# A drain, two orders of gathers, transposes and sums moved in a kernel of attention and routed experts

## The chip, the core and the metric

The kernel runs on one core of one Trainium2 chip. The metric is the device time in microseconds (us) of one execution. The engines have short names in the profile: PE is TensorE (PEld its weight loads), DVE is VectorE, ACT is ScalarE, POOL is GpSimd, SP is SyncE. A "q" behind a name means the engine's sequencer, which waits and issues DMAs.

## The reference

Eight batches of eight heads go through attention that is causal in blocks of 64 rows; the result, as rows of 512, goes through a layer of eight experts in which each row is sent to one expert.

```python
B, H, S, D = (8, 8, 576, 64)                       # attention
scores = scale * np.matmul(q, k.transpose(0, 1, 3, 2))
mask = block_i >= block_j                          # blocks of 64
attn = np.exp(scores - max) / (sum + 1e-09)
x = np.matmul(attn, v)                             # -> (B, S, 512)
...
logits = np.einsum('bsd,de->bse', x, w_gate)       # E = 8 experts, F = 1024
local_gate = sigmoid(x @ w_local)
for s in range(S):
    fresh_e = argmax(logits[b, s])
    e = fresh_e if s == 0 or local_gate[b, s] < 0.5 else prev_e
    h = np.maximum(x[b, s] @ w1[e], 0.0)
    out[b, s] = softmax(logits[b, s])[e] * (h @ w2[e])
```

## The kernel before

**First stage, attention.** The loop over `i` from 0 to 31 takes one pair of heads per slot (`NPAIR` is 32, `HP` is 4 pairs per batch). TensorE's order in slot `i` is written out by hand: the products with the values of the pair before (`values(i - 1)`, L932), the scores of this pair in three units (L894) with the last block of 64 (`last_scores`, L917), the transposes of keys and queries of the next pair (`transposes(i + 1)`: eight of 128 rows, L856, and one of the tail, the last 64 rows of keys and of queries, L860), and then what the slot has of tasks: gate logits, sums, turning the result back into rows, steps of the routing. Slots 1 and 3 have no tasks. Slot 1 has another order (`swap`): its scores come first, then the values of pair 0, then the transposes, then the sums.

ScalarE makes the exponentials (L904, L921), copies the eight transposed blocks from PSUM into `qkT` (L851; in slot 0 VectorE does that) and the output of the values out of `po` (L936). VectorE adds the exponentials of the column blocks into S (`add_chunks`, L944), so that one product with ones later gives the sums, and copies the tail (L862). GpSimd clears the corners above the diagonal (L881), rearranges the loaded keys and queries (L822) and issues the loads of the experts' weights. The PSUM tile `po` of 1024 columns is shared: columns 0 to 127 take the tail's transpose, 128 to 191 and 832 to 895 the scores of the last block, 256 to 831 the output of the values. The tiles named `sc` rotate through three buffers; scores, the eight transposes (`kq`) and the tasks take them in turn.

**The routing** (which row goes to which expert, at which place) is a generator of small steps, most of them VectorE's. `steps.vector(w)` issues steps until their written weights reach `w`; `steps.tensor()` issues one that needs TensorE. The steps of slot 25's end are `steps.vector(2.7)`, those at slot 26's start `steps.vector(1.4)` after the sums of pair 25.

**Second stage, the experts.** The rows are grouped in tiles of 128 with one expert each, 15 tiles of a first group (rows of the first five batches) and 28 of a second group whose row numbers are only known some time into this stage; of these 43, 38 run always and 5 stand behind a branch. For tile `i`: GpSimd gathers its rows from DRAM into `xg` (six buffers; L654), SyncE issues a transposing DMA into `xT` (L1218), VectorE copies the expert's first matrix (L1205), TensorE multiplies (L1006, 32 products), ScalarE applies the Relu (L1009), TensorE multiplies with the second matrix (L1155, 8 products), ScalarE scales the result into `y` (three buffers; L1160), and GpSimd stores it row by row with an indirect DMA (L1162). On TensorE the second matrix of tile `i - 1` follows the first of tile `i`. GpSimd's queue runs in program order. In the first group the order per iteration is: store of tile `i - 1`, then the gather of tile `i + 5`, which takes the buffer of tile `i - 1`. The gathers of tiles 0 to 3 are issued in the attention stage, those of 4 and 5 in iteration 0, and behind them stands `nc.gpsimd.drain()` (L1281), which holds GpSimd's queue until what is before it is done. A second drain stands before the branch (L1295). From the second group on the gather of tile `i + 4` stands ahead of the store.

SyncE's queue holds, in program order too, the loads, the stores of attention rows and of routing factors (L676, L680), and the transposing DMAs. The order around the gathers in an iteration of the second stage:

```python
gathers(i + AHEAD, relu[0] if i > NS[0] + 1 else None)
second_mm(*tiles[i - 1], done, ev.pop(i - 1), factor_of(xgs[(i - 1) % NX]))
...
if i < NS[0] + 1:
    gathers(i + NX - 1)
if i == 0:
    nc.gpsimd.drain()
if i + 2 >= AHEAD:
    rows_of(i + 2)
```

Here `AHEAD` is 4, `NX` 6 and `NS[0]` 15.

Of the kernel before, what the change touches and what calls it, by code (L numbers as in the profile page):

```python
# [62 lines left out]
def kernel(  # L63
# [11 lines left out]
    nc = tc.nc  # L75
# [14 lines left out]
    P = 128  # L90
# [119 lines left out]
    def factor_of(x):  # L210
        return x[:, XH:]
# [562 lines left out]
    with tc.tile_pool(name="atn_const", bufs=1) as cst, \  # L774
# [78 lines left out]

        def turn_part(i, part, ps):
            for j in range(4):
                nc.tensor.transpose(ps[:, j * P:j * P + P],  # L856
                                    raws[i][1 + part][:, j].rearrange("s h d -> s (h d)"), id_f)
# [6 lines left out]

        def transposes(i, copy):
            if i >= NPAIR:
                return
            ps = psp.tile([P, 2, 512], F32, tag="sc", name="kq")
            for part in range(2):
                turn_part(i, part, ps[:, part])  # L870
            back_in_order(i, slice(0, 2), ps, copy)
            turn_tail(i)

# [186 lines left out]
        wload = 0  # L1060

        def behind(i):

            values(i - 1)
            if not swap:
                add_chunks(i - 1)
            load_v(i + 1)
            steps.vector(1.4)

        for i in range(NPAIR):  # L1070
# [18 lines left out]
            for u in range(len(UNITS)):  # L1089
                exps(i, u, scores(i, u))  # L1090
                if u == 0:
                    last_scores(i)
                    if i == 0:
                        transposes(1, nc.vector.tensor_copy)
                        constants()
                        for h in range(2):
                            hs = slice(64 * h, 64 * h + 64)
                            nc.sync.dma_start(
                                out=wg2[hs, :, 16 * h:16 * h + E],
                                in_=moe_w_gate.rearrange("(p h d) e -> h d p e", h=2, d=D)[h])  # L1100
                            nc.sync.dma_start(
                                out=wg2[hs, :, 16 * h + E:16 * h + E + 1],
                                in_=moe_w_local.rearrange("(p h d) e -> h d p e", h=2, d=D)[h])
            if swap:
                behind(i)
            if i:
                transposes(i + 1, nc.scalar.copy)
            if swap:
# [14 lines left out]
            steps.tensor()  # L1123
            if i < NPAIR - 1:
                steps.vector(2.7)
# [9 lines left out]
        slot[0] = NPAIR  # L1135


        values(NPAIR - 1)
# [8 lines left out]
    with tc.tile_pool(name="ffn_s", bufs=2, reuse_waits="tile") as f_p, \  # L1147
# [3 lines left out]

        def second_mm(ph, j, hT, ev, factor, y=None):
            ps = f_ps.tile([P, Dm], F32, tag="ps_y", name="ps_y")
# [4 lines left out]
            if y is None:  # L1158
                y = f_p.tile([P, Dm], F32, tag="y", name="y", bufs=3)
            nc.scalar.activation(y, ps, func=AF.Copy, scale=factor)  # L1160

            st = nc.gpsimd.indirect_dma_start(  # L1162
# [51 lines left out]
        def rows_of(i):  # L1214

            if i < len(tiles):
                xT = f_p.tile([P, KO1, P], BF16, tag="xT", name="xT", bufs=3)
                ended["DMA", len(ended)] = nc.sync.dma_start(  # L1218
                    out=xT, in_=row_of_x(xgs[i % NX]), transpose=True)
                xTs[i] = xT  # L1220
# [39 lines left out]
        for i, (ph, j) in enumerate(tiles):  # L1260
# [10 lines left out]
            if i:  # L1271
                point()

                gathers(i + AHEAD, relu[0] if i > NS[0] + 1 else None)
                second_mm(*tiles[i - 1], done, ev.pop(i - 1), factor_of(xgs[(i - 1) % NX]))


            if i < NS[0] + 1:
                gathers(i + NX - 1)
            if i == 0:  # L1280
                nc.gpsimd.drain()  # L1281
            if i + 2 >= AHEAD:
# [54 lines left out]
```

## Time and profile before

| what | us |
|---|---|
| runs of the kernel | 432.31, 431.83, 432.20 |
| their median | 432.2 |
| the profiled execution, its own time | 433.36 |
| its span, from the first to the last instruction | 431.6 |
| granted TensorE clock over the span | 1.00 |

The profile is one execution. Its times are us from the start of the span. A row of the timeline gives start, duration, engine, line, operation, tiles and shapes, a count, and in brackets the idle time of the engine before it with the one who ended it. That name is inferred from semaphores: where an engine waits for several, the profile names the one that came last. Matmuls are pipelined, so neighbouring rows of TensorE overlap a little.

By stage (busy us of each engine; a view of stretches): the attention up to 280.6 us, the stretch to the row of TensorE that waits, that stretch, and the rest:

```profile
core 0: us, PE busy (x) PEld busy (x) DVE busy (x) ACT busy (x) POOL busy (x), PEclk, DMA share, GB/s
0.00:280.60 280.60, 276.71 (x2657) 203.22 (x2657) 179.89 (x411) 183.95 (x292) 87.53 (x237) 1.00 0.87 175
280.60:312.00 31.40, 30.94 (x349) 21.77 (x348) 26.33 (x82) 12.75 (x22) 13.48 (x11) 1.00 0.65 132
312.00:314.00 2.00, 0.43 (x8) 0.47 (x9) 1.97 (x5) 0.69 (x1) 1.70 (x2) 1.00 0.82 179
314.00:432.00 118.00, 112.04 (x1275) 81.41 (x1271) 47.14 (x63) 59.07 (x94) 83.86 (x61) 1.00 0.55 136
```

### The profile page before, as it was taken

The numbers are of one execution on the slowest core, as the hardware profiler recorded it, in microseconds if no ns is written. First come the engines' busy times: TensorE is split into PE (matmuls) and PEld (weight loads), VectorE is DVE, ScalarE is ACT, GpSimd is POOL, SyncE is SP. The second block draws the span as 40 slices with busy tenths as digits, with TensorE's granted clock in tenths as the row PEclk, the third lists the DMA queues.
The fourth block names the chain that finished last, engine by engine and source line by source line (L and its number), as shares of the span: only waits on it lengthen the run. The fifth ranks groups of instructions, "written<-read, shape, count | busy, mean of one in ns | idle before, by whom it ended". The sixth has DMA issues, their size and how long they took to land. (4 is left out here: it accounts for less than half of the span.)

```text
span 431.6 us, 11727 instructions
## 1 busy us (share of the span) xinstructions
PE 420.1 (97%) x4282; PEld 306.9 (71%) x4282; DVE 255.3 (59%) x557; ACT 256.5 (59%) x409; POOL 186.6 (43%) x309
## 2 busy tenths in 40 slices
PE   8999999999999999999999999999999999999995
PEld 7677767767677776676776777667677777777763
DVE  3353565466365566968789976898788433333320
ACT  4668657766776677656676557634444555555553
POOL 2324522232222223314223234304875788888843
PEclk9999999999999999999999999999999999999999
DMA  7568699799899789796989979993686465664541
GB/s 183 124 161 184 119 215 169 154 212 213 176 185 204 167 159 196 162 139 150 225 142 218 192 161 170 182 146 86 159 189 141 132 148 147 142 154 139 142 107 74
DMA packets 114360, 69.78 MB, mean 162 GB/s; under 512 B 77567, under 2 KB 106751, under 8 KB 114304
## 3 DMA queue, kind: packets, MB, share of 16 engines
q1 hardware_dynamic: 96896, 38.07, 39.1%
q0 software_dynamic: 17408, 30.96, 37.2%
q8 instruction: 36, 0.59, 0.6%
q14 instruction: 20, 0.16, 0.1%
HBM read 66.88 MB, written 14.70 MB: 189 GB/s over the span
## 5 line engine op out<-in xcount | busy, mean ns | idle before, releaser
L944 DVE TENSOR_TENSOR S<-S,Pc 128x896 f32<-128x896 f32 (+3 forms) x128 | 90.5, 707 | 16.9 <-PE o L932 8.7
L894 PE MATMUL sc<-qkT 64*128 64x288 f32 (+3 forms) x768 | 98.7, 389 | 0.4 <-ACT qkT L1054 0.3
L894 PEld LDWEIGHTS sc<-qkT 64*128 64x128 f32 x768 | 68.7, 187 | 14.1 <-ACT qkT L1054 0.5
L1205 DVE COPY w1c<-w_bf 128x4096 bf16 x36 | 44.4, 1232 | 55.4 <-PE ps_h L1006 52.2
L1006 PEld LDWEIGHTS <-w1c 128*128 128x128 bf16 x1152 | 67.2, 98 | 10.7 <-DVE x L765 2.0
L1162 POOL DMA_INDIRECT out_dram<-y,idx x38 | 60.2, 1584 | 28.4 <-ACT hT L1009 12.5
L1155 PE MATMUL ps_y<-w_bf,hT 128*128 x304 | 71.7, 379 | 0.0
L1006 PE MATMUL ps_h<-xT,w1c 128*128 128x128 bf16 x1088 | 66.3, 219 | 2.5 <-DMA xT<-xg 1.6
L936 ACT COPY oT<-o 128x576 f32<-128x576 f32 x32 | 20.5, 639 | 80.0 <-PE o L932 77.7
L904 ACT ACTIVATE Pc<-sc 128x448 f32<-128x448 f32 (+1 forms) x96 | 63.9, 707 | 0.0
L851 ACT COPY qkT<-kq 128x1024 f32<-128x1024 f32 x30 | 63.4, 2112 | 0.4 <-PE kq L856 0.4
L1009 ACT ACTIVATE hT<-ps_h 128x512 bf16<-128x512 f32 x76 | 45.2, 597 | 24.5 <-PE ps_h L1006 24.5
L932 PE MATMUL o<-Pc,v 128*64 128x320 f32 (+2 forms) x512 | 57.4, 366 | 0.0
L822 POOL COPY w_bf<-w_bf 128x512 f32<-128x512 f32 x61 | 41.8, 702 | 33.2 <-DMA w_bf<-in_k_dram 19.5
L654 POOL DMA_INDIRECT xg<-x_rows,idx x38 | 43.1, 1133 | 22.9 <-DVE w1c L1205 10.9
L1160 ACT ACTIVATE y<-ps_y,xg 128x512 f32<-128x512 f32 x38 | 26.2, 689 | 43.8 <-PE ps_y L1155 35.1
L932 PEld LDWEIGHTS o<-Pc,v 128*64 128x64 f32 x512 | 35.1, 137 | 23.6
L904 ACT ACTIVATE S<-sc 128x576 f32<-128x576 f32 x64 | 41.6, 650 | 15.3 <-PE sc L894 15.2
L1155 PEld LDWEIGHTS <-hT 128*128 128x128 bf16 x304 | 28.2, 98 | 27.7 <-issue 0.5
L881 POOL MEMSET Pc<- 64x128 f32 x96 | 17.5, 200 | 65.5 <-ACT Pc L904 61.2
L881 POOL MEMSET S<- 64x128 f32 x32 | 6.4, 199 | 91.0 <-ACT S L904 90.0
L862 DVE COPY qkT<-o 128x128 f32<-128x128 f32 x32 | 9.2, 288 | 55.2 <-PE o L860 55.0
(287 smaller groups left out, 453.1 us busy)
## 6 DMA issues: line engine op xcount, KB each, us to landing
w_bf<-in_moe_w_dram POOLq DMA_DIRECT2D x16, 1024.0 KB
w_bf<-in_k_dram SPq DMA_DIRECT2D x32, 256.0 KB, 4.2
w_bf<-in_q_dram SPq DMA_DIRECT2D x32, 256.0 KB, 4.2
v<-in_v_dram SPq DMA_DIRECT2D x64, 128.0 KB, 3.3
x_rows<-xg SPq DMA_DIRECT2D x24, 128.0 KB, 3.1
qkl<-in_k_dram SPq DMA_DIRECT2D x32, 32.0 KB, 3.4
qkl<-in_q_dram SPq DMA_DIRECT2D x32, 32.0 KB, 4.2
vl<-in_v_dram SPq DMA_DIRECT2D x32, 32.0 KB, 8.9
```

The lines of the kernel that those rows point to most:

```text
L654: st = nc.gpsimd.indirect_dma_start(out=x, out_offset=None, in_=x_dram[:rows], in_offset=bass.IndirectOffsetOnAxis(ap=row_of(ph, j), axis= ...
L822: copies[j](m, raws[i][1 + j].rearrange("p h j d -> p j h d"))
L851: copy(qkTs[i % 2][:, parts, :512].rearrange("p a (s j) -> p a j s", j=4), ps.rearrange("p a (j s) -> p a j s", j=4))
L894: nc.tensor.matmul(ps[:, h, col:col + n], lhsT=t[r, 0, c * P:c * P + P], rhs=t[r, 1, q0:q0 + n], start=True, stop=True)
L904: nc.scalar.activation(exps_at(i, c, q0, n, rows), ps[rows, :, col:col + n], func=AF.Exp, scale=scale_attn)
L932: nc.tensor.matmul(po[64 * h:64 * h + 64, VO + q0:VO + q0 + n], lhsT=vv, rhs=exps_at(i, c, q0, n, slice(0, P))[:, h, :], start=(c == 0), s ...
L944: nc.vector.tensor_add(Ss[i][rows, :, P * c:], Ss[i][rows, :, P * c:], Pc[i % 2][rows, :, POS[c]:POS[c] + n])
L1006: nc.tensor.matmul(ps[:, fo, :], lhsT=w[:, ko * F + f0:ko * F + f0 + P], rhs=xT[:, ko, :], start=(ko == 0), stop=(ko == KO1 - 1))
L1009: relu[0] = nc.scalar.activation(hT[:, half * (FO // 2):(half + 1) * (FO // 2), :], ps, func=AF.Relu)
L1155: nc.tensor.matmul(ps, lhsT=hT[:, fo, :], rhs=w2_bf[:, bass.ds(ev + fo * Dm, Dm)], start=(fo == 0), stop=(fo == FO - 1))
L1162: st = nc.gpsimd.indirect_dma_start(out=out_flat, out_offset=bass.IndirectOffsetOnAxis(ap=row_of(ph, j), axis=0), in_=y, in_offset=None, b ...
L1205: ended["w"] = nc.vector.tensor_copy(w, w1_bf[:, bass.ds(ev[i], WE)])
```

## The change

Five edits.

1. The transpose of the tail moves ahead of the eight others (`ahead` 0: first; 6 in slot 1: behind six of them; 8 in slot 0: behind all eight as before). VectorE's copy of the tail moves with it, and in slot 0 this copy now stands ahead of VectorE's copy of the eight.
2. The routing steps worth 2.7 at the end of slot 25 move to slot 26, behind the sums of pair 25.
3. GpSimd's first drain moves from behind the gathers of tiles 4 and 5 to a place ahead of the values of the last pair, that is ahead of these gathers.
4. In the first group the gather of tile `i + 5` stands ahead of the store of tile `i - 1`, behind ScalarE's scaling. The gathers of tiles 4 and 5 stay in iteration 0.
5. `xT` has five buffers instead of three.

```diff
@@ -851,8 +851,8 @@
             copy(qkTs[i % 2][:, parts, :512].rearrange("p a (s j) -> p a j s", j=4),
                  ps.rearrange("p a (j s) -> p a j s", j=4))
 
-        def turn_part(i, part, ps):
-            for j in range(4):
+        def turn_part(i, part, ps, js=range(4)):
+            for j in js:
                 nc.tensor.transpose(ps[:, j * P:j * P + P],
                                     raws[i][1 + part][:, j].rearrange("s h d -> s (h d)"), id_f)
 
@@ -862,14 +862,18 @@
             nc.vector.tensor_copy(qkTs[i % 2][:, :, 512:S],
                                   po[:, TAIL:TAIL + P].rearrange("p (a s) -> p a s", a=2))
 
-        def transposes(i, copy):
+        def transposes(i, copy, ahead=0):
             if i >= NPAIR:
                 return
             ps = psp.tile([P, 2, 512], F32, tag="sc", name="kq")
-            for part in range(2):
-                turn_part(i, part, ps[:, part])
+
+
+            for j in range(9):
+                if j == ahead:
+                    turn_tail(i)
+                if j < 8:
+                    turn_part(i, j // 4, ps[:, j // 4], (j % 4,))
             back_in_order(i, slice(0, 2), ps, copy)
-            turn_tail(i)
 
         def exps_at(i, c, q0, n, rows):
             if c == 0:
@@ -1059,12 +1063,17 @@
         arrange(1, (nc.vector.tensor_copy, nc.gpsimd.tensor_copy))
         wload = 0
 
+
+        SUMS_FIRST = 26
+
         def behind(i):
 
             values(i - 1)
             if not swap:
                 add_chunks(i - 1)
             load_v(i + 1)
+            if i == SUMS_FIRST:
+                steps.vector(2.7)
             steps.vector(1.4)
 
         for i in range(NPAIR):
@@ -1091,7 +1100,7 @@
                 if u == 0:
                     last_scores(i)
                     if i == 0:
-                        transposes(1, nc.vector.tensor_copy)
+                        transposes(1, nc.vector.tensor_copy, 8)
                         constants()
                         for h in range(2):
                             hs = slice(64 * h, 64 * h + 64)
@@ -1104,7 +1113,7 @@
             if swap:
                 behind(i)
             if i:
-                transposes(i + 1, nc.scalar.copy)
+                transposes(i + 1, nc.scalar.copy, 6 if swap else 0)
             if swap:
                 add_chunks(i - 1)
             for x in pending.pop(0) if pending else []:
@@ -1121,7 +1130,7 @@
                 w_next = weights_at(qkT.rearrange("p j a s -> p (j a s)").bitcast(BF16)[:, :WE],
                                     ev[1])
             steps.tensor()
-            if i < NPAIR - 1:
+            if i < NPAIR - 1 and i != SUMS_FIRST - 1:
                 steps.vector(2.7)
             arrange(i + 2, [nc.gpsimd.tensor_copy] * 2)
 
@@ -1135,6 +1144,8 @@
         slot[0] = NPAIR
 
 
+        nc.gpsimd.drain()
+
         values(NPAIR - 1)
         add_chunks(NPAIR - 1)
         steps.all()
@@ -1149,7 +1160,7 @@
                      reuse_waits="tile") as f_ps:
         banks["of"] = lambda nm: f_ps.tile([P, 512], F32, tag="rt", name=nm, bufs=3)
 
-        def second_mm(ph, j, hT, ev, factor, y=None):
+        def second_mm(ph, j, hT, ev, factor, y=None, between=lambda: None):
             ps = f_ps.tile([P, Dm], F32, tag="ps_y", name="ps_y")
             for fo in range(FO):
                 nc.tensor.matmul(ps, lhsT=hT[:, fo, :],
@@ -1158,6 +1169,7 @@
             if y is None:
                 y = f_p.tile([P, Dm], F32, tag="y", name="y", bufs=3)
             nc.scalar.activation(y, ps, func=AF.Copy, scale=factor)
+            between()
 
             st = nc.gpsimd.indirect_dma_start(
                 out=out_flat,
@@ -1214,7 +1226,7 @@
         def rows_of(i):
 
             if i < len(tiles):
-                xT = f_p.tile([P, KO1, P], BF16, tag="xT", name="xT", bufs=3)
+                xT = f_p.tile([P, KO1, P], BF16, tag="xT", name="xT", bufs=5)
                 ended["DMA", len(ended)] = nc.sync.dma_start(
                     out=xT, in_=row_of_x(xgs[i % NX]), transpose=True)
                 xTs[i] = xT
@@ -1272,13 +1284,12 @@
                 point()
 
                 gathers(i + AHEAD, relu[0] if i > NS[0] + 1 else None)
-                second_mm(*tiles[i - 1], done, ev.pop(i - 1), factor_of(xgs[(i - 1) % NX]))
-
-
-            if i < NS[0] + 1:
-                gathers(i + NX - 1)
-            if i == 0:
-                nc.gpsimd.drain()
+
+
+                second_mm(*tiles[i - 1], done, ev.pop(i - 1), factor_of(xgs[(i - 1) % NX]),
+                          between=lambda: i < NS[0] + 1 and gathers(i + NX - 1))
+            else:
+                gathers(NX - 1)
             if i + 2 >= AHEAD:
                 rows_of(i + 2)
 
```

## The prediction

> **What bounds the kernel now.** The page's busy line comes first, then the view of waits for TensorE alone: who it waited for, total us, times, longest us.
>
> ```profile
> span 431.6 us, 11727 instructions
> PE 420.1 (97%) x4282; PEld 306.9 (71%) x4282; DVE 255.3 (59%) x557; ACT 256.5 (59%) x409; POOL 186.6 (43%) x309
> ...
> PE ps_h L1006 <- DMA xT<-xg: 1.6, 1, 1.6
> PE ps_h L1006 <- ACTq L1297: 0.8, 1, 0.8
> PE rtr L364 <- ACT qkT L851: 0.8, 2, 0.4
> ...
> PE o L932 <- POOL w_bf L822: 0.4, 1, 0.4
> PE o L932 <- POOL Pc L881: 0.4, 1, 0.4
> ...
> PE trg L704 <- DVE S L944: 0.2, 1, 0.2
> ```
>
> TensorE is the bound from end to end: all its idle time is 431.6 - 420.1 = 11.5 us. The change removes no arithmetic, so it can gain only what stands in such rows, and it can lose by making new ones. Every term below is therefore a TensorE wait that goes, stays, or comes. Two rows are out of reach: the 0.8 us at L1297 is the branch near the end, which is not touched, and the chain of waits after TensorE's last product is not either.
>
> **The long wait, 1.57 us.** The timeline around it (start, us, engine, line; in brackets the idle time before and who ended it), with GpSimd's DMAs, ScalarE's first two y, the transposing DMA of tile 7 and the drain (its duration, then its start):
>
> ```profile
> 313.57 1.95 PE L1006 MATMUL ps_h<-xT,w1c 128*128 128x128 bf16 x32 [1.57 <-DMA xT<-xg]
> ...
> 308.17 1.21 SPq L1218 DMA_TRANSPOSE xT<-xg  x1
> ...
> 291.18 1.48 POOL L654 DMA_INDIRECT xg<-x_rows,idx  x1 [10.88 <-DVE w1c L1205]
> 292.96 1.00 POOL L654 DMA_INDIRECT xg<-x_rows,idx  x1 [0.30 <-issue]
> 298.56 1.02 POOL L1162 DMA_INDIRECT out_dram<-y,idx  x1 [4.60 <-ACT hT L1009]
> 299.89 1.02 POOL L654 DMA_INDIRECT xg<-x_rows,idx  x1 [0.30 <-issue]
> ...
> 303.44 1.02 POOL L654 DMA_INDIRECT xg<-x_rows,idx  x1 [0.30 <-issue]
> ...
> L1281 POOLq DRAIN  x1: 6135/6135/6135, 291.5 to 291.5; - x1
> ...
> 291.04 0.69 ACT L1160 ACTIVATE y<-ps_y,xg 128x512 f32<-128x512 f32 x1 [0.27 <-PE ps_y L1155]
> ...
> 295.44 0.69 ACT L1160 ACTIVATE y<-ps_y,xg 128x512 f32<-128x512 f32 x1 [1.13 <-PE ps_y L1155]
> ```
>
> The gathers of tiles 4 and 5 are issued at 291.18 and 292.96, and the second ends on GpSimd at 293.96. Then the drain holds the queue until 291.49 + 6.14 = 297.6, and the 4.60 us before the store at 298.56 are its price. The gather of tile 6 starts at 299.89, behind that store, and that of tile 7 at 303.44, behind the next. Tile 7 is the one TensorE stands waiting for: gathered at 303.44, sent to the transposing DMA at 308.17, used at 313.57, 10.13 us in all.
>
> After the change the drain stands before L1138 in GpSimd's order. There the engine is free: it did nothing in the 10.88 us before 291.18, that is from 280.30. A drain of 6.14 us from there ends at 286.4, under cover of a wait that ends at 291.18 anyway; if that cover went, each us beyond 291.18 would move the gathers of tiles 4 to 7 by as much. Then, with the gather ahead of the store in each tile: tile 6's gather needs its buffer, free when y of tile 0 is made (291.04 + 0.69 = 291.73), so it follows tile 5's at 293.96 + 0.30 = 294.26; the store of tile 0 takes 295.58 to 296.60; y of tile 1 is ready at 296.13, so tile 7's gather starts at 296.90, 6.5 us earlier. Even with the whole old lag of 10.13 us it is usable at 307.0, and TensorE wants it at 313.57 - 1.57 = 312.00. So the wait goes: **-1.57**. The stores move behind one gather of 1.02 us each; three y buffers cover that. With five xT buffers instead of three, SyncE's transpose of tile 7 needn't wait for the product that reads tile 4, so that the earlier gather is of use.
>
> **Tail first, where nothing stands between two slots.** Slots 1 and 3 have no tasks after the transposes, so the values of the pair follow at once, and there the two waits of 0.4 us sit:
>
> ```profile
> 33.39 1.09 PE L856 MATMUL kq<-id_f,w_bf 128*128 128x128 f32 x8
> 34.32 0.27 PE L860 MATMUL o<-id_f,qkl 128*128 128x128 f32 x1
> 34.63 0.29 DVE L862 COPY qkT<-o 128x128 f32<-128x128 f32 x1 [2.77 <-PE o L860]
> 34.78 0.34 POOL L881 MEMSET Pc<- 64x128 f32 x2 [1.89 <-ACT Pc L904]
> 34.99 0.23 PEld L932 LDWEIGHTS o<-S,v 128*64 128x64 f32 x4 [0.64 <-POOL Pc L881]
> ...
> 17.25 0.64 ACT L936 COPY oT<-o 128x576 f32<-128x576 f32 x1 [1.64 <-PE o L932]
> ...
> 18.38 0.29 DVE L862 COPY qkT<-o 128x128 f32<-128x128 f32 x1 [6.39 <-PE o L860]
> 18.74 0.23 PEld L932 LDWEIGHTS o<-S,v 128*64 128x64 f32 x4 [0.64 <-POOL w_bf L822]
> ```
>
> The profile names GpSimd as the releaser both times. I don't believe it: in both places the weight load starts 0.07 us after VectorE's copy of the tail ends (34.92 to 34.99, 18.67 to 18.74), while the first values product reads S, which these memsets of Pc don't write. Tail and values lie in the same tile `po`, columns 0 to 127 and 256 to 831. Turned ahead of the eight others the tail is ready (1.09 - 0.27)/7 = 0.12 us times eight, about 0.94, sooner, its copy ends near 34.0, and values run straight on: **-0.43** (bounds 0, if GpSimd is the true releaser, and -0.43).
>
> The Trainium skill, "PSUM — Partial Sum Buffer", section "PSUM bank collisions raise a hardware error", says that two engines must be kept apart by bank and quadrant and not by address; a bank holds 512 of these columns. By that rule the values have to wait for the copy of the tail, as the 0.07 us suggest, and the sum is as here; by the name in the bracket it would be 0.5 us less.
>
> In slot 1 the tail goes between the sixth and the seventh of the eight, so two places (0.24 us) sooner at most, and it can't start before ScalarE's copy out of `po` ends at 17.25 + 0.64 = 17.89: 0 to -0.24, I take **-0.10**.
>
> **Tail first, its costs.** In slot 0 the tail stays behind the eight, but VectorE now copies it ahead of the big copy:
>
> ```profile
> 9.01 0.28 PE L860 MATMUL o<-id_f,qkl 128*128 128x128 f32 x1
> 9.21 2.00 DVE L851 COPY qkT<-kq 128x1024 f32<-128x1024 f32 x1 [2.47 <-PE kq L856]
> ...
> 11.27 0.30 PEld L894 LDWEIGHTS sc<-qkT 64*128 64x128 f32 x4 [0.34 <-DVE qkT L851]
> ```
>
> The scores of pair 1 already wait for that copy (0.34 before 11.27), so nothing covers it. It starts after the tail's product ends (9.29, not 9.21) and after a copy of 0.29: 0.08 + 0.29 = 0.37 at most, at least 0.2 if the two overlap; **+0.34**. From here on the waits of the later slots follow TensorE, so it is carried through.
>
> In the other slots the eight end one place, 0.12 us, later, and so may ScalarE's copy of them:
>
> ```profile
> 32.53 0.32 ACT L921 ACTIVATE Pc<-o 64x64 f32<-64x64 f32 x2
> 33.27 1.46 ACT L904 ACTIVATE Pc<-sc 128x448 f32<-128x448 f32 x2
> 34.60 2.14 ACT L851 COPY qkT<-kq 128x1024 f32<-128x1024 f32 x1
> ```
>
> ScalarE is busy up to 34.73 when the copy begins, and the eight end at 34.48, so either may hold it. Values cover the copy in nearly all slots. Only the two waits of 0.4 us at L364 end with it: 0 to +0.12 each, I take 0.09, **+0.18** for both.
>
> **Slot 26.**
>
> ```profile
> 232.06 3.35 DVE L944 TENSOR_TENSOR S<-S,Pc 128x896 f32<-128x896 f32 x4
> ...
> 236.41 0.28 DVE L862 COPY qkT<-o 128x128 f32<-128x128 f32 x1
> ```
>
> The sums of pair 25 end at 235.41, and the products that read them wait 0.2 us. With about 2 us of routing steps behind them instead of ahead, that wait goes. But VectorE does the same total before the tail's copy, which now ends at 236.69 and gates the next values: between 0 and -0.20, **-0.15**, since VectorE gets the tail a little sooner.
>
> **The sum.** -1.57 - 0.43 - 0.10 + 0.34 + 0.18 - 0.15 = -1.73 us. The profiled execution took 433.36 us with a span of 431.6; it would take 431.6 with a span of 429.9. The median of the runs was 432.2, so the forecast is **430.5**.
>
> **Rivals.** First, *the wait moves to the second group's first tile*. Its row numbers come out of VectorE's chain:
>
> ```profile
> 334.63 0.21 DVE L603 TENSOR_TENSOR S<-S,rti 128x56 f32<-128x56 f32 x1 [0.22 <-PE rti L597]
> ...
> 335.33 0.19 DVE L433 SCALAR_TENSOR_TENSOR idx<-S 128x28 int32<-128x28 f32 x1
> 335.79 1.39 POOL L654 DMA_INDIRECT xg<-x_rows,idx  x1 [0.51 <-DVE idx L433]
> ...
> 343.19 1.95 PE L1006 MATMUL ps_h<-xT,w1c 128*128 128x128 bf16 x32
> ...
> DMA to landing us min/median/max: 2.6/3.3/4.8
> ```
>
> From gather to use there were 343.19 - 335.79 = 7.40 us, and they were enough, but the last row (the transposing DMA of all tiles) lets its part vary by 2.2 us, so the slack is anything from 0 to 2.2. For it: if the chain stayed where it is, TensorE, 1.57 sooner, would lose up to 1.57 here. Against it: the chain's last link waits for TensorE (0.22), so it moves along. If 1.4 of the 1.57 is lost here, the time is 431.9. Chance 0.14.
>
> Second, *GpSimd is the true releaser* in slots 2 and 4: the 0.53 stays, 431.0. Chance 0.08.
>
> Third, *the change doesn't do what it says*: tile 7 comes as late as before. The drain would be one way, if it met the last load of weights still moving:
>
> ```profile
> 273.85 0.98 POOL L111 DMA_DIRECT2D w_bf<-in_moe_w_dram  x1
> ```
>
> Tile 7's gather may start at 312.00 - 10.13 = 301.87 without a wait, 4.97 after the 296.90 above, so the drain would have to end 4.97 us after 291.18 to bring the wait back and 6.5 after it to bring all of it back, which is 23.8 us after that load's issue. The other way is SyncE's queue, in which tile 7's transpose stands behind stores of rows that wait for VectorE. Then only the rest of the sum is left, -0.16: 432.0. Chance 0.08.
>
> Fourth, *slower*: the tail, now first, writes into `po` while ScalarE still reads there. It reads the last block's scores until 32.53 + 0.32 = 32.85, and TensorE comes to the transposes at 33.39: 0.54 to spare. If the tail's wait reaches beyond that, every one of 29 slots pays; from 1.73/29 = 0.06 us per slot beyond the margin on, the kernel is slower, and at 0.1 it is 432.2 - 1.73 + 2.9 = 433.4. Against it: ScalarE's block follows TensorE's, so the margin moves with both. Chance 0.08.
>
> **The numbers.** Forecast 0.62. Its own terms span -2.3 to -1.2, so 429.9 to 431.0; the range takes in rivals one to three: 429.7 to 432.1. About 0.2% (0.86 us, below 431.34) is what a measurement of this kernel can tell from none. Faster: 0.62 + 0.08 + 0.06 of the first rival = 0.76. Same: the rest of the first and the third, 0.16. Slower 0.08.
>
> **What would show it.** Right: no idle time before tile 7's product; the drain off the place after tile 5's gather, tile 6's gather near 294 and tile 7's near 297; values in slot 4 at once behind the transposes; the copy in slot 0 about 0.3 later. Wrong: a new wait for xT, above all at tile 15; tail products with idle time before them; the 0.43 still there.

## The result, and the profile after

The changed kernel takes 431.16 us in the median of 22 runs; 22 runs of the kernel before, beside them on the same chip, took 432.98. The ratio is 0.9964 with a 95% interval from 0.9948 to 0.9980, that is 1.6 us less, between 0.9 and 2.3. The two profiled executions differ by more: 433.36 and 430.77 us, with spans of 431.6 and 429.0.

The page's first lines after, and its view of TensorE's waits (who waited for whom, total us, times, longest us):

```profile
span 429.0 us, 11713 instructions
PE 419.5 (98%) x4282; PEld 306.6 (71%) x4282; DVE 255.6 (60%) x557; ACT 259.3 (60%) x409; POOL 186.4 (43%) x309
...
PE rtr L364 <- ACT qkT L851: 0.9, 2, 0.5
...
PE sc L898 <- DVE sel L793: 0.5, 1, 0.5
...
PE o L936 <- issue: 0.2, 1, 0.2
```

TensorE's idle time fell from 11.5 to 9.5 us. The wait for `xT` is gone, nothing waits for `xT` at the second group's first tile either, one of the two waits of 0.4 us for the values is gone and the other is halved; the routing products wait 0.9 instead of 0.8, and the scores of pair 1 have a wait of their own. (Lines behind the transposes stand a few numbers later than before: scores L898, values L936, sums L948, GpSimd's clearing L885, first product L1010.)

GpSimd's queue where the experts begin, with the drain, the transposing DMA of tile 7, the first product of tile 6 and that of tile 7, from the timeline and the view of one line:

```profile
L1147 POOLq DRAIN  x1: 8512/8512/8512, 279.1 to 279.1; - x1
...
290.21 1.61 POOL L654 DMA_INDIRECT xg<-x_rows,idx  x1 [10.74 <-DVE w1c L1217]
292.12 1.00 POOL L654 DMA_INDIRECT xg<-x_rows,idx  x1 [0.30 <-DMA x_rows<-factors]
293.43 1.00 POOL L654 DMA_INDIRECT xg<-x_rows,idx  x1 [0.30 <-issue]
...
296.07 2.02 POOL L654 DMA_INDIRECT xg<-x_rows,idx  x1 [0.30 <-issue]
...
300.78 1.20 SPq L1230 DMA_TRANSPOSE xT<-xg  x1
...
306.99 1.95 PE L1010 MATMUL ps_h<-xT,w1c 128*128 128x128 bf16 x32
310.95 1.95 PE L1010 MATMUL ps_h<-xT,w1c 128*128 128x128 bf16 x32
```

In the kernel before, the first product of tile 6 starts at 307.87, and that of tile 7, which waits, at 313.57.

The four gathers of tiles 4 to 7 start at 290.21, 292.12, 293.43 and 296.07; tile 7's was forecast for 296.90 and stood at 303.44 before. The drain is longer than before (8.51 against 6.14 us) but ends at 287.6, 2.6 ahead of the first of them.

Slot 4, where the 0.43 us were, in the timeline:

```profile
34.30 0.29 DVE L862 COPY qkT<-o 128x128 f32<-128x128 f32 x1 [1.90 <-PE o L860]
35.06 1.19 PE L936 MATMUL o<-S,v 128*64 128x256 f32 x8
35.32 0.35 POOL L885 MEMSET Pc<- 64x128 f32 x2 [1.88 <-ACT Pc L908]
```

The values start at 35.06, with no bracket, while GpSimd's clearing, which the profile of before named as the releaser, starts only at 35.32. So it isn't what held the values up. The tail's copy, which now ends at 34.59, is left; the experiments on slot 26 bear that out.

Slot 0, where a loss was forecast: scores of pair 0, the copies, the scores of pair 1 that wait for them, the values of pair 0; first after, then before.

```profile
6.63 1.13 PE L898 MATMUL sc<-qkT 64*128 64x288 f32 x8 [0.31 <-ACT qkT L1058]
9.52 0.29 DVE L862 COPY qkT<-o 128x128 f32<-128x128 f32 x1 [2.43 <-PE o L860]
9.73 1.99 DVE L851 COPY qkT<-kq 128x1024 f32<-128x1024 f32 x1
11.86 1.13 PE L898 MATMUL sc<-qkT 64*128 64x288 f32 x8 [0.45 <-DVE sel L793]
14.88 1.19 PE L936 MATMUL o<-S,v 128*64 128x256 f32 x8
```

```profile
6.43 1.13 PE L894 MATMUL sc<-qkT 64*128 64x288 f32 x8 [0.31 <-ACT qkT L1054]
...
8.52 0.66 PE L856 MATMUL kq<-id_f,w_bf 128*128 128x128 f32 x4 [0.19 <-POOL w_bf L822]
...
14.28 0.65 PE L932 MATMUL o<-S,v 128*64 128x256 f32 x4
```

From the first scores to the first values it is 8.25 us after and 7.85 before. The bracket again names something small of VectorE's (clearing `sel`) that stands behind the big copy.

And the part whose term was far too small, slot 26: gate products (L704), values, and after also the tail's copy; before, then after.

```profile
234.55 0.71 PE L704 MATMUL trg<-S,sel 128*32 128x320 f32 x6
235.47 1.26 PE L704 MATMUL trg<-S,sel 128*32 128x320 f32 x10 [0.20 <-DVE S L944]
236.79 1.19 PE L932 MATMUL o<-S,v 128*64 128x256 f32 x8
```

```profile
235.51 0.28 DVE L862 COPY qkT<-o 128x128 f32<-128x128 f32 x1
...
234.78 1.26 PE L704 MATMUL trg<-S,sel 128*32 128x320 f32 x16
235.97 1.19 PE L936 MATMUL o<-S,v 128*64 128x256 f32 x8
```

The 16 products took from 234.55 to the values at 236.79, 2.24 us, and now 1.19. The view of waits showed 0.20 of the difference. Before, the stretch broke: six products, a wait for the sums, ten more in 1.26 us, as long as all sixteen take after.

**Where the time lies, over all profiles.** Fourteen profiles are compared. Each column is the difference of two start times in TensorE's timeline: *slot 0*, first scores to first values; *slot 2* and *slot 4*, values of pair 0 to those of pair 1, and of pair 2 to pair 3; *19*, *23*, values of pairs 18 to 19 and 22 to 23 (the routing products at L364); *26*, values of pair 25 to pair 26; *tile 7*, first product of tile 6 to first product of tile 7, the one that waited.

| kernel | slot 0 | slot 2 | slot 4 | 19 | 23 | 26 | tile 7 |
|---|---|---|---|---|---|---|---|
| before | 7.85 | 4.49 | 7.50 | 9.42 | 9.31 | 9.80 | 5.70 |
| before, again | 7.53 | 4.49 | 7.50 | 9.40 | 9.30 | 10.28 | 3.96 |
| before, one copy sooner | 7.53 | 4.49 | 7.50 | 9.41 | 9.30 | 10.76 | 3.96 |
| before + GpSimd's part | 7.53 | 4.49 | 7.50 | 9.41 | 9.32 | 9.79 | 3.96 |
| before + drain moved | 7.53 | 4.49 | 7.50 | 9.40 | 9.30 | 9.56 | 3.96 |
| before + order of gathers | 7.53 | 4.49 | 7.50 | 9.41 | 9.30 | 9.20 | 3.95 |
| before + attention part | 8.25 | 4.43 | 7.00 | 9.52 | 9.39 | 10.36 | 3.95 |
| after | 8.25 | 4.43 | 7.00 | 9.50 | 9.38 | 8.76 | 3.96 |
| after, again | 8.24 | 4.42 | 7.00 | 9.50 | 9.38 | 9.05 | 3.96 |
| after, sums last | 8.25 | 4.43 | 7.00 | 9.49 | 9.38 | 9.77 | 3.96 |
| after, tail last | 8.24 | 4.49 | 7.50 | 9.41 | 9.32 | 9.65 | 3.96 |
| after, three slots back | 7.53 | 4.43 | 7.00 | 9.41 | 9.30 | 8.76 | 3.96 |
| the same, copy behind the sums | 7.53 | 4.42 | 7.00 | 9.43 | 9.30 | 8.76 | 3.96 |
| after, no first drain | 8.24 | 4.42 | 7.00 | 9.50 | 9.38 | 8.76 | 3.95 |

Five columns hardly vary between executions (7.85 in the first row apart): they give the edits' own prices. Slot 26 varies, and tile 7 has one row that stands out. The largest term of the prediction stood there: of the four profiles with GpSimd's queue as before, one has the long wait. In two of the other three TensorE came 3 to 5 us late to that place for other reasons.

### The profile page after: what moved, and what is told of

Read it like the earlier page. It is cut to its first block, busy times and chain, and to the rows that moved or that the text cites. A ratio compares the mean times of both kernels' runs of the same rounds, so it can differ in the third digit from the quotient of the medians.

```text
span 429.0 us, 11713 instructions
## 1 busy us (share of the span) xinstructions
PE 419.5 (98%) x4282; PEld 306.6 (71%) x4282; DVE 255.6 (60%) x557; ACT 259.3 (60%) x409; POOL 186.4 (43%) x309
## 4 chain that ended last, share of the span: by engine, by line
PE 84%; ACT 5%; DMA 5%; issue 2%; DVE 2%; POOL 1%; POOLq 0%; DVEq 0%
PE o L936 21%; PE sc L898 18%; PE ps_h L1010 12%; PE ps_y L1166 11%; PE trg L704 6%; PE kq L856 6%; DMA out_dram<-y,idx 5%; PE trx L718 3%; ACT Pc L908 2%; PE o L860 2%; PE trl L726 1%; ACT S L908 1%; PE o L921 1%; ACT qkT L851 1%; PE idle L1031 1%
## 5 line engine op out<-in xcount | busy, mean ns | idle before, releaser
L948 DVE TENSOR_TENSOR S<-S,Pc 128x896 f32<-128x896 f32 (+3 forms) x128 | 90.7, 709 | 17.3 <-PE o L936 6.6
L898 PE MATMUL sc<-qkT 64*128 64x288 f32 (+3 forms) x768 | 98.7, 389 | 0.8 <-DVE sel L793 0.5
L898 PEld LDWEIGHTS sc<-qkT 64*128 64x128 f32 x768 | 69.0, 187 | 14.3 <-PE sc L898 0.7
L1010 PEld LDWEIGHTS <-w1c 128*128 128x128 bf16 x1152 | 67.1, 98 | 9.0 <-DVE w1c L1217 1.8
L1010 PE MATMUL ps_h<-xT,w1c 128*128 128x128 bf16 x1088 | 66.3, 219 | 1.0 <-PEq L1019 0.8
L1174 POOL DMA_INDIRECT out_dram<-y,idx x38 | 55.8, 1467 | 22.6 <-issue 9.8
L654 POOL DMA_INDIRECT xg<-x_rows,idx x38 | 48.1, 1267 | 26.3 <-DVE w1c L1217 10.7
L936 PE MATMUL o<-Pc,v 128*64 128x320 f32 (+2 forms) x512 | 57.3, 366 | 0.0
L936 PEld LDWEIGHTS o<-Pc,v 128*64 128x64 f32 x512 | 34.7, 137 | 23.9
L885 POOL MEMSET Pc<- 64x128 f32 x96 | 17.5, 200 | 65.8 <-ACT Pc L908 61.7
L885 POOL MEMSET S<- 64x128 f32 x32 | 6.4, 199 | 88.0 <-ACT S L908 87.0
L936 PE MATMUL o<-S,v 128*64 128x256 f32 (+1 forms) x256 | 38.1, 418 | 0.2 <-issue 0.2
```

The source lines that it names most:

```text
L654: st = nc.gpsimd.indirect_dma_start(out=x, out_offset=None, in_=x_dram[:rows], in_offset=bass.IndirectOffsetOnAxis(ap=row_of(ph, j), axis= ...
L898: nc.tensor.matmul(ps[:, h, col:col + n], lhsT=t[r, 0, c * P:c * P + P], rhs=t[r, 1, q0:q0 + n], start=True, stop=True)
L936: nc.tensor.matmul(po[64 * h:64 * h + 64, VO + q0:VO + q0 + n], lhsT=vv, rhs=exps_at(i, c, q0, n, slice(0, P))[:, h, :], start=(c == 0), s ...
L948: nc.vector.tensor_add(Ss[i][rows, :, P * c:], Ss[i][rows, :, P * c:], Pc[i % 2][rows, :, POS[c]:POS[c] + n])
L1010: nc.tensor.matmul(ps[:, fo, :], lhsT=w[:, ko * F + f0:ko * F + f0 + P], rhs=xT[:, ko, :], start=(ko == 0), stop=(ko == KO1 - 1))
L1174: st = nc.gpsimd.indirect_dma_start(out=out_flat, out_offset=bass.IndirectOffsetOnAxis(ap=row_of(ph, j), axis=0), in_=y, in_offset=None, b ...
```

## The experiments

Each is a change to one of the two kernels. Ratios are to the kernel before, run beside it on the same chip. Times on the chip of numbers 5, 10, 11 and 12 are some 5 us longer throughout, the kernel before's too, so there only ratios and stretches are compared.

**1 to 3. GpSimd's part in pieces.** All GpSimd's edits in the kernel before; the drain's place alone; the order of gathers (with five `xT`) alone.

```diff
+        nc.gpsimd.drain()
         values(NPAIR - 1)
...
-            if i == 0:
-                nc.gpsimd.drain()
```

```diff
-                second_mm(*tiles[i - 1], done, ev.pop(i - 1), factor_of(xgs[(i - 1) % NX]))
...
-            if i < NS[0] + 1:
-                gathers(i + NX - 1)
+                second_mm(..., between=lambda: i < NS[0] + 1 and gathers(i + NX - 1))
+            else:
+                gathers(NX - 1)
```

> The kernel before with the GpSimd part alone: drain moved, gathers ahead of stores in the first group, five xT buffers. Theory (this part is worth the 1.57 us of the wait before tile 7's product and nothing else): that wait is gone, the other TensorE waits stay as before (0.43 twice near 18.3 and 34.6 us, 0.40 twice at the routing products, the sums' wait in slot 26), span about 1.6 us shorter than before, 430.0. Rival (the gain of the profiled span, 2.6 us, comes mostly from here, through DMA traffic that is ordered otherwise): span near 429.0.

> The kernel before with the drain moved ahead of the last values and nothing else; the store stays ahead of the gather and xT has three buffers. Theory (the drain alone was what made tile 7 late): its gather starts near 298 instead of 303.4, 298 + 10.1 is before 312, the wait of 1.57 us is gone. Rival (the order of store and gather is needed too): a wait of some tenths to 1.57 us before tile 7's product is left.

> The kernel before with gathers ahead of stores and five xT buffers; the drain stays behind the gathers of tiles 4 and 5. Theory: the drain still ends near 297.6, but the gathers follow it at 298 and, behind one store, at 300.6; 300.6 + 10.1 is 310.7, before 312, so the order alone takes the wait away too, with little to spare. Rival (the drain has to go): a wait before tile 7's product is left, up to 1.57 us.

Measured: 431.69 us, 0.9970 (0.9954 to 0.9986); 431.66 us, 0.9967 (0.9946 to 0.9988); 431.90 us, 0.9993 (0.9974 to 1.0013). In none of the three does TensorE wait before tile 7. The first has a span of 430.2 us, as the theory had it (430.0) and not its rival (429.0). The gather of tile 7 with the drain alone, then the gathers of tiles 6 and 7 with the order alone:

```profile
298.59 1.02 POOL L654 DMA_INDIRECT xg<-x_rows,idx  x1 [0.30 <-issue]
```

```profile
297.82 0.99 POOL L654 DMA_INDIRECT xg<-x_rows,idx  x1 [4.12 <-issue]
...
300.45 1.38 POOL L654 DMA_INDIRECT xg<-x_rows,idx  x1 [0.30 <-issue]
```

With the drain moved tile 7's gather starts at 298.59; with the drain left where it was (the 4.12 before 297.82 are its price) and the gather ahead of the store, at 300.45. Either is before the 301.87 that the prediction gave as the latest, so each edit alone brings tile 7 in time, as the theories had it; the five buffers aren't needed for it, since the run with the drain alone had three. This rests on the gathers' times: that the wait is missing says little, since most profiles with the old queue lack it too, and by its time the order alone can't be told from the kernel before.

**4. The attention part alone.** The changed kernel with GpSimd's three edits undone.

> The kernel before with the attention part alone: tail first and sums first in slot 26. Theory: the 1.57 us wait before tile 7's product stays; slot 0 loses about 0.4, slots 2 and 4 gain 0.2 and 0.43, the two routing products lose 0.08 each, slot 26 gains 1.05 (the shift between the two traces there, not the 0.20 of the view of waits); together -1.1 us, span 430.5. Rival (slot 26 gains only the 0.15 to 0.20 of the prediction): together -0.2 us, span 431.4.

Measured: 431.87 us, 0.9978 (0.9964 to 0.9992), that is 0.95 us less (0.35 to 1.56): the theory's 1.1 lies in it, the rival's 0.2 doesn't. Slots 0, 2, 4, 19 and 23 are as in the changed kernel. Two things were not expected. From its timeline:

```profile
234.87 0.30 PE L860 MATMUL o<-id_f,qkl 128*128 128x128 f32 x1 [1.55 <-DMA qkl<-in_q_dram]
...
302.09 1.76 POOL L654 DMA_INDIRECT xg<-x_rows,idx  x1 [0.30 <-issue]
...
305.96 2.33 SPq L1228 DMA_TRANSPOSE xT<-xg  x1
...
312.76 1.95 PE L1010 MATMUL ps_h<-xT,w1c 128*128 128x128 bf16 x32
```

In slot 26 the tail, now first, met its load before it had landed: 1.55 us. In the six other profiles with the tail first in that slot this load was in time. And with GpSimd's queue in the order of before there is no wait before tile 7: its gather started 1.35 sooner than in before's profile and was handed to the transposing DMA after 3.87 us, not 4.73, while TensorE came 0.76 later (312.76 against 312.00).

**5. The kernel before, again.** Unchanged, one execution.

> The kernel before once more, for a second profile of it. Theory: the long wait before tile 7's product hangs on the lateness of tile 7's gather, which the drain sets, and on how long the transposing DMA takes (5.3 us from issue to use in the first profile of before, 2.6 to 3.3 us in most others), so it need not be in every execution: here 0 to 1.6 us, and if it is there, the gather starts at 303 us or later and the transposing DMA takes over 4 us. Rival: it comes with GpSimd's order alone; then 1.5 to 1.6 us again, and its absence in the run that had only the attention part was due to that part. In slot 26 the values start at the later of two times: 0.36 us after the last product of the gate starts, and 0.10 us after VectorE's copy of the tail ends.

Measured: a time of 436.97 us beside a median of 437.37. Tile 7, and slot 26:

```profile
303.60 1.02 POOL L654 DMA_INDIRECT xg<-x_rows,idx  x1 [0.30 <-issue]
...
307.33 1.84 SPq L1218 DMA_TRANSPOSE xT<-xg  x1
...
315.11 1.95 PE L1006 MATMUL ps_h<-xT,w1c 128*128 128x128 bf16 x32
...
236.53 0.28 DVE L862 COPY qkT<-o 128x128 f32<-128x128 f32 x1
236.91 1.19 PE L932 MATMUL o<-S,v 128*64 128x256 f32 x8 [0.56 <-POOL w_bf L822]
```

The gather is as late as in the first profile of before (303.60 against 303.44), but it was handed on after 3.73 us, and TensorE, held up elsewhere on this chip, came to tile 7 only at 315.11. So there is no wait, and this execution doesn't say whether there would be one with TensorE on time: had it come at 312.00, and had tile 7 taken as long from the transposing DMA to its use as in the first profile (308.17 to 313.57, 5.40 us), some 0.7 us would have been left, by this estimate. In number 4 tile 7 was handed on 2.21 sooner than in before's profile, more than the 1.57, so by the same estimate it came in time there even for 312.00. GpSimd's order alone thus doesn't bring the wait each time. But number 4 carries the attention part, to which the rival puts the missing wait down; whether that part made the gather sooner stays open. Slot 26 obeys the rule of the expectation: the copy ends at 236.81, the values start at 236.91.

**6. Sums last again.** The changed kernel with the routing steps of 2.7 back at the end of slot 25.

```diff
-        SUMS_FIRST = 26
+        SUMS_FIRST = NPAIR + 1
```

> The changed kernel with the routing sums of slot 26 where they were before (ahead of none of the routing steps moved). Theory of the prediction: that part is worth 0.15 us, so the time is 431.3 us, ratio 0.9968 to before, and the start of the values of pair 26 lies 0 to 0.6 us earlier than in before when measured from the values of pair 25, as in the runs whose attention code is that of before (0.0, 0.24, 0.61). Rival: the whole 1.05 us by which slot 26 was shorter in the first profile of the changed kernel is due to the sums: then 432.2 us, ratio 0.9988, no shortening of slot 26, and the wait of 0.2 us of the products at L704 for the sums is back.

**7. Tail last again.** The changed kernel with the tail behind the eight in slots 1 to 28.

```diff
-                transposes(i + 1, nc.scalar.copy, 6 if swap else 0)
+                transposes(i + 1, nc.scalar.copy, 8)
```

> The changed kernel with the tail turned last again in slots 1 to 28 (slot 0 keeps VectorE's new order of copies). Theory: the values of slot 4 wait 0.43 us again and those of slot 2 0.4 us, the two routing products at L364 wait 0.4 instead of 0.47 us each, so 0.5 us more than the changed kernel: 431.65 us, ratio 0.9975. The scores of pair 1 in slot 0 still come 0.35 to 0.45 us late. Rival: the tail first costs something in many slots that no single wait shows; then this kernel is faster than the changed one, 430.9 us or less, ratio 0.9958 or less.

Measured, on one chip with numbers 8 and 9: sums last 431.41 us, 0.9980 (0.9959 to 1.0002); tail last 432.11 us, 0.9985 (0.9963 to 1.0008). By the time neither can be told from the changed kernel (number 9: 431.49), so the profiles decide. Slot 26 with the sums last, then with the tail last (a row at the end of a view counts only the products inside it):

```profile
232.07 3.40 DVE L948 TENSOR_TENSOR S<-S,Pc 128x896 f32<-128x896 f32 x4
236.88 0.28 DVE L862 COPY qkT<-o 128x128 f32<-128x128 f32 x1
...
235.05 1.73 PE L704 MATMUL trg<-S,sel 128*32 128x320 f32 x16
237.26 1.15 PE L936 MATMUL o<-S,v 128*64 128x256 f32 x7 [0.47 <-issue]
```

```profile
237.03 0.28 DVE L862 COPY qkT<-o 128x128 f32<-128x128 f32 x1
...
237.41 0.92 PE L936 MATMUL o<-S,v 128*64 128x256 f32 x6 [0.82 <-POOL w_bf L822]
```

With the sums last the 16 products are stretched from 1.26 to 1.73 us by sums that end at 235.47, and then the values wait for the tail's copy (237.16 to 237.26). With the tail last the sums are early, but the copy ends only at 237.31, and the values start 0.10 later. Slot 26 is 9.77 and 9.65 us long, no shorter than without any of the change (9.20 to 10.28); only with both it is 8.76 to 9.05 (the 10.36 of number 4 holds the 1.55 of its late load). My theory, 0.15 us for the sums, is refuted by the trace. Its rival had the slot right, no shortening without the sums, but not the cause, since number 7 shows that the sums alone don't bring the 1.05. The rival of number 7, a time of 430.9 or less, falls. The tail last also gives back the 0.50 of slot 4 and the 0.07 of slot 2 and takes 0.09 and 0.06 off the routing products.

**8. Three slots put back.** In slot 0 VectorE copies the eight first again; in slots 19 and 23 the tail is last.

```diff
             back_in_order(i, slice(0, 2), ps, copy)
+            if ahead == 8:
+                turn_tail(i)
...
-                transposes(i + 1, nc.scalar.copy, 6 if swap else 0)
+                transposes(i + 1, nc.scalar.copy, 6 if swap else 8 if i in (19, 23) else 0)
```

> The changed kernel with three slots as before: in slot 0 VectorE copies the eight ahead of the tail again, and in slots 19 and 23 (those with the routing products at L364) the tail is turned last. Theory: the 0.37 us of slot 0 and 0.08 us at each of the two products come back, 0.5 us less than the changed kernel: 430.65 us, ratio 0.9952; scores of pair 1 wait as in before (0.1 us or less beyond its 0.34), L364 0.40 and 0.39. Rival: what is won in slot 0 is lost at the next wait that does not move with TensorE (a load of q, k or v, or ScalarE), and the time equals that of the changed kernel, 431.1 to 431.2, ratio 0.9964.

**9. The changed kernel, again.**

> The changed kernel once more, for its spread and a second profile. Theory: 431.2 us, ratio 0.9950 to 0.9980; no wait before the product of tile 7 nor of tile 15; 0.4 us more before the scores of pair 1; values of slot 4 without a wait. Slot 26 tells whether the 1.05 us of the first profile belong to the change: theory says that part of them is run to run, so 0.2 to 0.9 us here; the rival says 1.05 again.

Measured: three slots back 430.42 us, 0.9946 (0.9929 to 0.9964); the changed kernel again 431.49 us, 0.9969 (0.9952 to 0.9986). The first scores of pair 0, VectorE's copy of the eight, the tail's product and the first values in the version with three slots back:

```profile
6.71 1.13 PE L899 MATMUL sc<-qkT 64*128 64x288 f32 x8 [0.33 <-DVE w_bf L822]
...
9.07 1.99 DVE L851 COPY qkT<-kq 128x1024 f32<-128x1024 f32 x1 [2.36 <-PE kq L856]
9.23 0.33 PE L860 MATMUL o<-id_f,qkl 128*128 128x128 f32 x1 [0.20 <-ACT Pc L926]
...
14.23 0.65 PE L937 MATMUL o<-S,v 128*64 128x256 f32 x4
```

Slot 0 takes 7.53 us, 0.72 less than in the changed kernel, and 0.32 less than in the first profile of before, whose transposes waited for keys still being rearranged (the 0.19 above). With 0.09 and 0.08 at the routing products this makes 0.89 us; the medians differ by 1.07. The copy of the eight starts 2.36 us after the first scores here (6.71 to 9.07) and 3.10 in the changed kernel (6.63 to 9.73): the tail's product, which waits 0.20 us for ScalarE's reading of `po`, starts only after that copy, and the tail's copy starts later still. The rival (the gain lost again at a later wait) falls. This is the fastest version; its interval overlaps the changed kernel's, so the lead rests on the medians of one chip and on the stretches.

**10. One copy sooner, in the kernel before.** In slot 26 the tail's copy ahead of the five last routing steps.

```diff
             load_v(i + 1)
-            steps.vector(1.4)
+            if i != 26:
+                steps.vector(1.4)
...
                 transposes(i + 1, nc.scalar.copy)
+            if i == 26:
+                steps.vector(1.4)
```

> The kernel before with one move: in slot 26 VectorE's copy of the tail stands ahead of the five last routing steps (L425 to L426, 1.07 us in before), with the sums where they were. Theory (the values of a slot wait for that copy, whatever name the profile puts in the bracket): the values then start 0.36 us after the last product of the gate, not 0.47 to 1.06 us as in the four profiles with the sums last, so slot 26 is 0.1 to 0.7 us shorter, and the time some 0.3 us below before: 432.6 us, ratio 0.9993, not to be told from 1 by the time alone. Rival (the copy doesn't matter, only the sums do): values still 0.47 us or more behind the last product.

Measured: 0.9996 (0.9968 to 1.0025). The profile doesn't decide. The slot's transposes waited twice, 1.2 and 0.5 us, for keys and queries that came late; the first of the two:

```profile
234.46 0.66 PE L856 MATMUL kq<-id_f,w_bf 128*128 128x128 f32 x4 [1.16 <-POOL w_bf L822]
```

so the gate products came after both the sums and the copy. The values start 0.36 behind the last product, as both would have it then.

**11. The same in the version of number 8**, with the copy ahead of all thirteen steps.

```diff
-            if i == SUMS_FIRST:
-                steps.vector(2.7)
-            steps.vector(1.4)
+            if i != SUMS_FIRST:
+                steps.vector(1.4)
...
+            if i == SUMS_FIRST:
+                steps.vector(2.7)
+                steps.vector(1.4)
```

> The version with three slots put back (slot 0's copies, tail last in slots 19 and 23), and in slot 26 VectorE's copy of the tail right behind the sums, ahead of the thirteen routing steps. Theory: values of slot 26 start 0.36 us behind the last product of the gate in every execution, against 0.36 to 0.66 in the profiles with the sums first, so 0 to 0.3 us below the version with three slots: 430.3 us, ratio 0.9943. Rival: the routing steps, now 0.3 us later, hold up the products that read them (L341, L364, or the next gate), and the time is 0.3 us or more above it.

Measured: 0.9956 (0.9922 to 0.9990), not to be told from 0.9946. The copy now ends at 233.35, 2.2 us ahead of the values, and slot 26 is 8.76 us. That is what number 8 had already, so nothing was left to win there in these executions. VectorE's routing steps, now behind the copy, run on to 236.03 while the values start at 235.58, so the values don't wait for the rest of VectorE's queue.

**12. No first drain.** The changed kernel without it.

```diff
-        nc.gpsimd.drain()
         values(NPAIR - 1)
```

> The changed kernel without the first drain of GpSimd; the second one stays. Theory: the drain's 8.5 us lay wholly under the wait for the lists of rows, so taking it away changes nothing: 431.2 to 431.5 us, ratio 0.9964 to 0.9972, gathers of tiles 4 and 5 at the same time after the lists as with it. Rival: the drain still holds something up; then 0.5 us or more faster, 430.8 us or less.

Measured: 1.0016 (0.9978 to 1.0054). Neither theory expected a time no shorter than before. The first gather starts at 290.03 (290.21 with the drain), so the drain held nothing up there. The loss is elsewhere in its profile; its longest wait:

```profile
PE rtb L341 <- DVE S L338: 2.4, 1, 2.4
```

Stalls of this kind are in other profiles of this chip too (2.2 us in number 10 at L364, 2.2 in number 11 near the branch, where the bracket names VectorE's copy of a matrix), with the drain in its old or its new place. The changed kernel itself wasn't run on this chip. Whether the missing drain adds to such stalls, and why, stays open.

## Why the prediction was nearly right, point by point

The forecast was 430.5 us from a start of 432.2. The shift forecast was 1.73 us and 1.6 came; the range held the time. But the sum came out through wrong sizes of opposite sign, above all slot 0 and slot 26, and that it came so near is in part luck.

- **The wait before tile 7, -1.57.** The mechanism is as put: the drain and the store ahead made the gather late, and either edit takes it away. Where the wait is, it costs 1.74 (5.70 against 3.96), since without it the product starts 0.16 before the end of the one ahead of it (310.95 against 311.11 in the changed kernel). What the prediction left out is that the wait isn't there in each execution: it came where a late gather, a slow passage to the transposing DMA (4.73 us against 3.87, 3.73 and 3.60) and a TensorE on time met. The times say that it is no rarity: GpSimd's part alone gains 1.3 us (0.6 to 2.0), and its profile differs from before's in nothing else that is steady. At 1.74 for each wait that would be some three executions in four (one in three to all of them, by the interval), or shorter waits in more. This share is worked out, not shown.
- **Slot 4, -0.43.** Right: 7.50 to 7.00 in all seven profiles with the tail first in slot 3, and 7.50 in all seven without. That the tail's copy in `po` and not GpSimd is the releaser is shown by the clearing that now starts after the values, and by slot 26, where in the profiles with a wait the values begin 0.10 us behind the end of that copy (237.16 and 237.26, 237.31 and 237.41, 236.81 and 236.91), whatever the bracket names. It agrees with the section of the Trainium skill on bank collisions, in "PSUM — Partial Sum Buffer", as the prediction read it: the two engines are kept apart although their columns differ. Whether they are kept apart by bank or by the whole tile `po` no run separates.
- **Slot 2, -0.10.** It gave 0.07. The wait in the bracket fell by twice as much, from 0.43 to 0.21; but with the tail between the sixth and the seventh of the eight the products themselves take longer. A wait that shrinks is not yet time won.
- **Slot 0, +0.34.** Mis-sized: 0.40 between the two profiles, and 0.72 against the 7.53 us of all other profiles with the old order. The working started from a profile that had lost 0.32 there already, and counted 0.08 us from the end of the eight to that of the tail's product; in number 8 that product ends 0.49 after VectorE's copy of the eight has started (9.56 and 9.07), and with the tail's copy first that counts as well as the tail's copy of 0.29.
- **Routing products, +0.18.** Right: 0.09 and 0.08.
- **Slot 26, -0.15.** The mis-sized term: 1.04 between the profiles, and about 0.9 against the 9.7 us that the five profiles with this part as before have in the mean (9.80, 10.28, 9.79, 9.56, 9.20). I had priced the one wait that the view named, 0.20. Two gates stand one behind the other: late sums break the rounds of the sixteen products, and the tail's copy, behind VectorE's queue, holds up the next values. Sums first moves the one, the tail first the other. The prediction named both, but thought that "VectorE does the same total before the tail's copy", and left out that with the tail first VectorE also comes to the slot's work sooner: 2.64 us after the values of pair 25 in the changed kernel (227.22 to 229.86), 3.04 with the tail last (227.76 to 230.80).

Summed by the steady columns the change costs 0.72 + 0.17 and saves 0.07 + 0.50 + 0.9, 0.6 us in all. With the 1.3 of GpSimd's part this makes 1.9, within the interval of what was measured, 0.9 to 2.3. A late load as in number 4 is not counted in this. In the two profiles the tile 7 wait counts in full, which is in the main why they lie 2.6 us apart.

The rivals: the second group's first tile has no wait in any profile; GpSimd as the true releaser is refuted; the drain ended 2.5 to 3.1 us ahead of the first gather in all eight profiles with it moved; and by the views of waits ScalarE's reading of `po` held the tail up in slot 0 alone, 0.20 us, where the tail isn't first. The rival on the slower side missed the real hazard of the tail being first: its load, 1.55 us late in one profile of seven.

## What to carry to other kernels

Take a second profile of the unchanged kernel before pricing a long wait: compare the stretches between the same two instructions, and keep those prices that don't move from one execution to the next. A named releaser is a guess; an end that is followed after the same short time in several profiles is evidence. And price a broken group of interleaved products by the whole stretch from its first product to what follows it, not by the wait that stands in the bracket.

## What the hardware showed that was not expected

- A drain of GpSimd has no fixed length. Behind the two gathers it took 6.14 to 6.74 us in five profiles; in the attention stage, ahead of them, 6.26 to 8.51 in eight. Those eight started at 278.3 to 280.6 and ended at 285.2 to 287.8. What ends a drain was not tried.
- Four of the stretches of the attention stage (slots 2, 4, 19 and 23) repeat to 0.03 us across chips with the same edits in place (slot 4: 7.50 or 7.00 in fourteen profiles), while VectorE's small steps don't: the same step L425 took 0.19 us in one profile and 0.61 in another. Such steps stand ahead of the tail's copy in slot 26, which moves with them.
